# A state-space scan and a low-rank mixer on one core: Up of batches 2 and 3 in blocks of 512 tokens, and a new order of the work

## The chip, the cores and the metric

The kernel runs on one core of a Trainium2 chip. The metric is the device time of one execution in microseconds, the median of several executions. Before the change it is 219.8 us (three runs, 219.1 to 220.63).

## What is computed

The reference has two parts, one fed by the other. There are 4 batches, 8 heads, 768 tokens, head width 32 and state width 16; the mixer's model width is 256, its rank 32 and its hidden width 1024.

```python
# scan, in chunks of 32 tokens
cum = np.cumsum(log_a[:, :, sl], axis=-1)
L = np.exp(cum[:, :, :, None] - cum[:, :, None, :]) * causal
y_intra = (einsum('bhin,bhjn->bhij', C, B) * L) @ x
y_inter = einsum('bhin,bhnd->bhid', C, state) * np.exp(cum)[..., None]
state = exp(sum(log_a)) * state + sum_j(B_j x_j * exp(cum[-1] - cum_j))
y = y_intra + y_inter
# mixer, on y as (batch, token, 256)
h = y^T @ U @ V                      # over tokens, rank 32
u = y + h^T
out = u + max(u @ w_ch1, 0) @ w_ch2  # 256 -> 1024 -> 256: "Up" and "Down"
```

## The kernel before

All engines follow one list, PLAN (line 41). Each word of it is a step, and every step issues its instructions on the engines that it uses, so each engine's queue holds its own share of the steps in the order of the list. A step that waits holds up what lies behind it on its own engine only. `follow` (line 937) reads the list.

The scan works on 12 pieces of 256 tokens, three to a batch, numbered 0 to 11. The words of piece k are: `Bk`, `Xk` loads (with a leading Y where nothing holds them back), `Pk` or `Qk.c` the scaling of B and C by decays on the vector engine (DVE), `Tk` or `Vk...` the transposes on the tensor engine (PE) with their copies on the scalar engine (ACT), `gk` the products C times B (line 544), `mk` and `Mk` the causal mask on DVE (a tile M), `sk` the products for the state (line 578), `uk` the state's update on DVE and its masked copy on GpSimd (POOL), `ik` the part that comes in from earlier pieces (line 658), `nk` and `jk` the part inside the piece (line 694), `yk` the copy out, `tk` or `Ok` the transposes back into token order (line 721).

The mixer's words carry the batch b: `pb`, `qb`, `ab.j` make the low-rank part and add it. The channel mixer then works in blocks of tokens. Before the change every block has 384 tokens, two to a batch. `Sb.j` splits the block's u into three parts (one ACT and two DVE instructions); `fb.j.m` is Up: for one of 8 groups of 128 hidden channels it makes 6 products (3 parts by 2 halves of the width) of 384 columns in a bank of PSUM, which ACT reads once with a relu; `hb.j.m` reads the same bank once on DVE and, at every odd m, joins two results with a DVE instruction of 768 columns; `db.j.k.n` is Down: 4 products of 256 columns, six such words for each 128 tokens of the block, the last with one product more and the sum and the store of the output. The products of Up and Down are issued at line 809. Block 0 of batch 0 is done in plain fp32 (`U`, and four `d` words to 128 tokens).

Weights come in with `w`, `YU`, `YV`, are converted by `c` and `C`, and split by `R`. `v0` (`spread`, line 893) lays V out over the partitions with 16 small products.

`E` words issue fill products (line 140), which compute nothing that is used: `En` is n times a product of a 128-wide identity with itself in fp32, in a bank of its own that it takes in its turn. One instruction covers up to four such units. I call one n a unit below.

PSUM has eight banks; the string BANKS names the bank for each use in turn. SLOTS does the same for 15 scratch tiles in SBUF of 1024 words a partition (`words`), in which loads, conversions, and the results of Up live. A bank or a slot is taken again only when its last reader is done. The loads are issued from SyncE's queue (SP).

Of the kernel before, what the change touches and what calls it, by code (L numbers as in the profile page):

```python
# [15 lines left out]
PLAIN = 1  # L16
BANKS = (
    '01720345670012367400561273334612337423057406175233406175234061752304237562137054713054762167'
    '2305417351473512603512476305143051247626241762405761357204615304712530471240653206127346126731'
    '26705706254317062705647031520312304504153761021072016325040375403')  # L20
SLOTS = (
    'abcdefghijklmnocaefbdgihmecjbldkagofhimncjekandeblmneogmfcmhjiakdbnolefhmgcadjnbeilofkhjcmdeal'
    'gibfonmkjeclhbagfidnkomlej')
# [55 lines left out]
def kernel(  # L79
# [113 lines left out]
    a_sb = const.tile([NB * NH * NC // 2, 2, P], FP32)  # L193
# [46 lines left out]
    Vn = const.tile([P, NC * RK], FP32R)  # L240
    Vs = const.tile([P, S], FP32R)
# [67 lines left out]
    ones = const.tile([P, P], FP32)  # L309
# [18 lines left out]
    upto = triangle("upto", const.tile([P, P], FP32, name="upto"), [[1, P]], 0, -1)  # L328

    low = [triangle("low", const.tile([P, P], FP32, name=f"low{v}"), [[0, P]], 31 + 64 * v, -1)  # L330
# [3 lines left out]
    ref = const.tile([P, P], FP32)  # L334
# [10 lines left out]
    nc.gpsimd.tensor_copy(out=spot, in_=same[:, None, :].to_broadcast([P, 4, Q]))  # L345
    mine = const.tile([P, NH], FP32)
# [19 lines left out]
    middle = const.tile([P, P], FP32)  # L366
    vector.tensor_tensor(out=middle, in0=low[1], in1=low[0], op=ALU.subtract)
    high = const.tile([P, P], FP32)
# [4 lines left out]

    F = const.tile([P, NB, NPR, NH, 2, 2], FP32)
# [28 lines left out]
    def keep(bs, tag="w"):  # L403
# [9 lines left out]
        own = att.tile([P, NB, J, NH], FP32, tag="own", name="own", bufs=1)[:, :n]  # L413
# [322 lines left out]

    def mixer(b):
        uT = yT[b]
        ps = mix.tile([P, DM], FP32R, tag="ps", name="ps")
        hold = {}  # L740
# [38 lines left out]

        def block(n, k):  # L780
            return uT[:, n, ts(k, HS)]
# [17 lines left out]
        def split(j):  # L799

            u = uT[:, :, ts(j, HS)]
            t = mix.tile([P, 3, NCB, HS], FP32R, tag="u", name="u", bufs=1)
            us[j] = [t[:, i] for i in range(3)]
            nc.scalar.activation(us[j][0], u, AF.Copy, scale=NEAR)
            halves(*us[j], u)
# [7 lines left out]
        def pair(dtype):  # L813
            t = words()
            return t.bitcast(dtype)[:, :2 * HS].rearrange("p (m t) -> p m t", m=2)

        def plain(j, m):

            if (j, m // 2) not in gT:
                gT[j, m // 2] = pair(FP32)  # L820
            t = bank("xz"[m % 2], HS)
            products(t, [(w1f[m // 2][:, n, ts(m % 2, P)], block(n, j)) for n in range(NCB)], True)
            nc.scalar.activation(gT[j, m // 2][:, m % 2], t, AF.Relu, scale=1.0 / MORE)

        def up(j, m):

            if (j, m // 2) not in gs:
                gs[j, m // 2] = [pair(FP32R)]
            gs["t", j, m] = t = bank("xz"[m % 2], HS)
            products(t, [(w1[v][:, n, ts(m, P)], us[j][v][:, n])  # L830
                         for v in range(3) for n in range(NCB)], True)
            gs["of", j, m] = behind["turn"]
            nc.scalar.activation(gs[j, m // 2][0][:, m % 2], t, AF.Relu, scale=NEAR)  # L833

        def third(j, m):

            g = gs[j, m // 2]
            if len(g) == 1:
                g.append(pair(FP32R))
# [5 lines left out]
            if m % 2:  # L845
                g.append(pair(FP32R))
                joined(*g)

        def down(j, k, n):

            parts = b or j >= PLAIN
            pieces = 6 if parts else 4
# [4 lines left out]
            if n == 0:  # L857
                gs["o", j, k] = bank("xzx"[k], DM)
            t = gs["o", j, k]
            c = HS // P * j + k  # L860
            if parts:
# [3 lines left out]
            else:  # L865
                products(t, [(gT[j, n][:, m, ts(k, P)], w2f[n][:, m]) for m in range(2)], n == 0)
            if n == pieces - 1:
                products(t, [(Vs[:, ts(c, P)], ps)], False)
                o = ytok[b][:, c]
                stored.append(c)  # L870
                if b < NB - 1 or len(stored) < NC:
                    behind.setdefault("part", summed(o, t, o))
                    nc.sync.dma_start(out=out[b, ts(c, P)], in_=o)
                else:
                    for queue, cols in ((nc.sync, ts(0, P)), (nc.scalar, ts(1, P))):
                        summed(o[:, cols], t[:, cols], o[:, cols])
                        queue.dma_start(out=out[b, ts(c, P), cols], in_=o[:, cols])

        us, gs, gT, stored = {}, {}, {}, []
# [6 lines left out]

    def convert(c, scalar=False):

        if c not in steps:
            steps[c] = to_fp32(*weights[c], c - 2 - NQ, scalar)  # L890
        next(steps[c])

    def spread():

        nc.scalar.copy(out=Vn, in_=Vq)
        vector.tensor_tensor(out=Vq, in0=Vq, in1=Vn.bitcast(FP32), op=ALU.subtract)
        v = [bank(tag, NC * RK) for tag in "yyxz"]
        for q in range(4):
            for i in range(4):
                rows = ts(i, Q)  # L900
                nc.tensor.matmul(out=v[i][ts(q, Q)], lhsT=ident[rows, rows],
                                 rhs=Vq[rows] if q % 2 else Vn[rows].bitcast(FP32),
                                 start=True, stop=True, skip_group_check=True)
# [88 lines left out]
```

## Time and profile before

| | |
|---|---|
| median of three runs | 219.8 us |
| profiled execution, its own time | 221.66 us |
| span of the profiled execution | 219.9 us |
| mean granted clock of the tensor engine | 0.977 |
| PE busy | 211.3 us (96%) |
| DVE busy | 150.1 us (68%) |
| ACT busy | 87.6 us (40%) |
| POOL busy | 35.4 us (16%) |
| read from and written to memory | 10.98 MB, 3.15 MB |

The span runs from the first to the last instruction. A busy share on PE counts an instruction from its start to a modelled end, so many small products that overlap can fill a stretch without the array being full; how densely PE works is seen better in the steps from the start of one product to the start of the next. The granted clock is the share of full speed at which the array ran.

### The profile page before, as it was taken

The numbers are of one execution on the slowest core, as the hardware profiler recorded it, in microseconds if no ns is written. First come the engines' busy times: TensorE is split into PE (matmuls) and PEld (weight loads), VectorE is DVE, ScalarE is ACT, GpSimd is POOL, SyncE is SP. The second block draws the span as 40 slices with busy tenths as digits, with TensorE's granted clock in tenths as the row PEclk, the third lists the DMA queues.
The fourth block names the chain that finished last, engine by engine and source line by source line (L and its number), as shares of the span: only waits on it lengthen the run. The fifth ranks groups of instructions, "written<-read, shape, count | busy, mean of one in ns | idle before, by whom it ended". The sixth has DMA issues, their size and how long they took to land.

```text
span 219.9 us, 7021 instructions
## 1 busy us (share of the span) xinstructions
PE 211.3 (96%) x3058; PEld 186.8 (85%) x3058; DVE 150.1 (68%) x314; ACT 87.6 (40%) x196; POOL 35.4 (16%) x52
## 2 busy tenths in 40 slices
PE   7879989998999999999999999999999999999994
PEld 3646756666778989999999988999999999999993
DVE  4737796787768899789653779746518776647532
ACT  2342736567574555443053531236342222323000
POOL 3011023368570740001000101200000000000000
PEclk9965999999999999999999999999999999999999
DMA  5989584678686850203210301000000000100012
GB/s 94 107 121 133 121 139 110 143 217 216 135 117 118 132 62 3 48 16 82 29 51 3 72 3 48 30 3 1 3 0 24 30 23 0 48 16 11 0 53 93
DMA packets 69663, 14.58 MB, mean 66 GB/s; under 512 B 63808, under 2 KB 67840, under 8 KB 69632
## 3 DMA queue, kind: packets, MB, share of 16 engines
q1 hardware_dynamic: 69488, 14.06, 32.6%
q8 instruction: 24, 0.39, 0.8%
q10 hardware_dynamic: 144, 0.07, 0.1%
q14 instruction: 7, 0.06, 0.1%
HBM read 10.98 MB, written 3.15 MB: 64 GB/s over the span
## 4 chain that ended last, share of the span: by engine, by line
PE 86%; DVE 6%; SPq 3%; DMA 1%; issue 1%; POOL 1%; DVEq 0%; POOLq 0%
PE x L809 38%; PE z L809 27%; PE y L694 4%; SPq L210 3%; PE y L658 3%; PE x L544 2%; PE w L504 2%; DVE words L182 2%; PE w L721 2%; PE w L140 2%; DMA bc<-in_C_dram 1%; PE w L578 1%; DVE M L182 1%; DVE S L182 1%; PE w L747 1%
## 5 line engine op out<-in xcount | busy, mean ns | idle before, releaser
L182 DVE SCALAR_TENSOR_TENSOR words<-words 128x768 fp32r<-128x768 f32 (+3 forms) x39 | 35.9, 919 | 5.1 <-PE z L809 3.4
L809 PE MATMUL x<-w,words 128*128 128x256 f32 x224 | 34.4, 284 | 0.0
L809 PE MATMUL x<-u,w 128*128 128x384 f32 x168 | 33.9, 340 | 0.0
L809 PE MATMUL z<-u,w 128*128 128x384 f32 x168 | 33.0, 340 | 0.0
L833 ACT ACTIVATE words<-x 128x384 fp32r<-128x384 f32 x28 | 13.8, 492 | 44.0 <-PE x L809 43.9
L809 PEld LDWEIGHTS x<-w,words 128*128 128x128 f32 x224 | 30.5, 190 | 0.2 <-issue 0.2
L809 PEld LDWEIGHTS z<-u,w 128*128 128x128 f32 x168 | 29.1, 188 | 0.3
L809 PEld LDWEIGHTS x<-u,w 128*128 128x128 f32 x168 | 28.8, 188 | 0.4 <-issue 0.2
L809 PE MATMUL x<-w2c,words 128*128 128x256 f32 x144 | 25.2, 305 | 0.0
L833 ACT ACTIVATE words<-z 128x384 fp32r<-128x384 f32 x28 | 13.7, 491 | 25.3 <-PE z L809 25.3
L809 PEld LDWEIGHTS x<-w2c,words 128*128 128x128 f32 x144 | 21.1, 189 | 1.1 <-issue 0.4
L182 DVE SCALAR_TENSOR_TENSOR words<-z,words 128x384 fp32r<-128x384 f32 x28 | 15.4, 551 | 9.0 <-ACT words L833 8.9
L809 PE MATMUL z<-w,words 128*128 128x256 f32 x112 | 18.4, 287 | 0.0
L182 DVE SCALAR_TENSOR_TENSOR words<-x,words 128x384 fp32r<-128x384 f32 x28 | 14.9, 551 | 4.0 <-ACT words L833 3.8
L605 POOL TENSOR_TENSOR Sm<-S,own 128x256 f32<-128x256 f32 (+1 forms) x12 | 7.2, 602 | 61.6 <-DVE S L182 61.6
L809 PEld LDWEIGHTS z<-w,words 128*128 128x128 f32 x112 | 15.7, 190 | 0.2
L694 PEld LDWEIGHTS y<-M,x 64*32 64x32 f32 x768 | 8.7, 113 | 5.9 <-POOL settled L617 2.8
L694 PE MATMUL y<-M,x 64*32 64x64 f32 x768 | 12.0, 237 | 1.5 <-POOL settled L617 1.3
L809 PE MATMUL z<-w2c,words 128*128 128x256 f32 x72 | 13.2, 307 | 0.0
L182 DVE SCALAR_TENSOR_TENSOR S<-S,kept,w 128x64 f32<-128x64 f32 x40 | 11.2, 280 | 2.6 <-PE w L504 0.5
L182 DVE TENSOR_TENSOR M<-x,causal 128x256 int32<-128x256 int32 x24 | 9.0, 416 | 5.7 <-PE z L544 4.3
L182 DVE SCALAR_TENSOR_TENSOR ytok<-x,ytok 128x256 f32<-128x256 f32 (+1 forms) x17 | 6.8, 407 | 7.3 <-PE x L809 7.3
(137 smaller groups left out, 337.3 us busy)
## 6 DMA issues: line engine op xcount, KB each, us to landing
words<-in_moe_w_ch_dram SPq DMA_DIRECT2D x7, 512.0 KB, 5.3
x<-in_x_dram SPq DMA_DIRECT2D x24, 128.0 KB, 3.2
out_dram<-ytok SPq DMA_DIRECT2D x23, 128.0 KB, 1.7
bc<-in_B_dram SPq DMA_DIRECT2D x24, 64.0 KB, 3.2
bc<-in_C_dram SPq DMA_DIRECT2D x12, 128.0 KB, 3.3
words<-in_moe_w_ch_dram SPq DMA_DIRECT2D x2, 256.0 KB, 3.0
words<-in_moe_U_dram SPq DMA_DIRECT2D x1, 192.0 KB, 3.5
words<-in_moe_V_dram SPq DMA_DIRECT2D x4, 48.0 KB, 2.5
```

The source lines that it names most:

```text
L140: nc.tensor.matmul(out=t[:, :m * P].rearrange("p (m i) -> p m i", i=P), lhsT=ident, rhs=ident[:, None, :].to_broadcast([P, m, P]), start=T ...
L182: self.last = call(*args, **kwargs)
L210: op = issuer[0].dma_start(**kwargs)
L504: nc.tensor.transpose(out=tp[:, i, v], in_=s["BC"][:, i, c + v].rearrange("p h n -> p (h n)"), identity=ident)
L544: nc.tensor.matmul(out=s["g"][r][cols, c], lhsT=s["T"][rows, 0, c, cols], rhs=s["Cm"][rows, :, :, ts(2 * c + p, Q)].rearrange("r v t i -> ...
L578: nc.tensor.matmul(out=s["A"][p][ts(r, Q), v], lhsT=s["BC"][half, 0, v, 2 * r:2 * r + 2].rearrange("p h n -> p (h n)"), rhs=x_sb[k][half, ...
L605: nc.gpsimd.tensor_tensor(out=s["Sm"][:, sl], in0=s["S"][:, sl].rearrange("p i (s d) -> p i s d", s=2), in1=own2[:, b, 4 * q + sl.start:4 ...
L658: nc.tensor.matmul(out=channels(k)[r // 2][ts(r % 2, H), c, p], lhsT=own[ts(r, Q)], rhs=st[k]["T"][ts(r, Q), 1, :, ts(2 * c + p, Q)].rearr ...
L694: product = nc.tensor.matmul(out=y[n][ts(i, Q), c, p], lhsT=x_sb[k][half, c, h], rhs=s["M"][half, h // 2, c, h % 2], start=fresh(k, n, [i] ...
L721: nc.tensor.transpose(out=t[:, c, g], in_=yT[b][:, g, ts(2 * q + c, P)], identity=ident)
L809: nc.tensor.matmul(out=t, lhsT=lhsT, rhs=rhs, start=start, stop=True, skip_group_check=True)
L833: nc.scalar.activation(gs[j, m // 2][0][:, m % 2], t, AF.Relu, scale=NEAR)
```

## The change

The list and the strings of banks and slots are new as a whole. Both openings, up to the first word of Up:

```python
# before
    'YX0 A0 YB0 Q0.0 YB1 A1 Q0.2 Q0.1 K0 s0 YB2 YB3 Q1.0 V0.0.0 V0.1.1 Q1.2 YU0 YX1 Q1.1 u0 '
    'Q2.0 E1 Q2.2 g0 m0 V1.0.2 B5 M0 V1.1.2 w0 V2.0.2 E2 n0 j0 g1 YX2 YV0 m1 i0 E1 P3 E1 M1 Q2.1 c0 '
    's1 n1 u1 c0 T3 T3 E2 V2.1.3 c1 P5 j1 y0 i1 g2 m2 w1 O0.0 s2 c1 B4 y1 T5 u2 M2 T5 g3 C0 m3 i2 '
    'n2 E1 X3 c0 j2 M3 y2 C0 c2 t1 C0 w3 c2 O2.1 v0 p0 s3 P4 T4 u3 X4 q0 c2 w2 T4 g5 a0.0 M5 X5 c4 '
    'w5 m5 n3 c1 U0.0.1 U0.0.0 ...'
# after
    'YX0 YB0 A1 A0 E1 Q0.0 YB1 E2 Q0.2 Q0.1 V0.0.0 V0.1.1 YX1 Q1.0 K0 YB2 s0 Q1.2 g0 E1 V1.0.2 Q1.1 '
    'm0 YX2 V1.1.2 s1 u0 E3 M0 B5 g1 E1 m1 n0 E2 M1 i0 Q2.0 Q2.1 j0 s2 y0 w0 YB3 u1 w1 Q2.2 n1 '
    'V2.0.2 P5 E4 YU0 V2.1.3 u2 YV0 T5 j1 w5 T5 c1 X3 B4 O0.0 g2 m2 i1 M2 i2 y1 P3 t1 c2 T3 c0 E1 '
    'c2 w2 T3 c0 n2 c1 E3 X4 w3 C0 X5 C0 E1 j2 c2 c1 w6 g3 m3 y2 R0 O2.1 E1 C0 E2 v0 c6 M3 c0 p0 g5 '
    'E1 M5 s3 w4 u3 q0 P4 n3 a0.0 i3 T4 m5 c6 R0 T4 U0.0.1 ...'
```

All fill words lie in these stretches: 6 words with 8 units before, 13 words with 23 units after. The words of Up for batches 2 and 3 go from 32 `f` words to 24, and their splits from four to three. The other words are the same ones in a new order, apart from the numbering of `d` words, of which there are 138 in both. The rest of the diff:

```diff
+BLOCKS = {(2, 0): [(2, 0, 512)], (2, 1): [(2, 512, 256), (3, 0, 256)], (3, 0): [(3, 256, 512)]}
...
-    a_sb = const.tile([NB * NH * NC // 2, 2, P], FP32)
+    early_on = [words().bitcast(FP32) for n in range(2)]
+    squares = iter([early_on[0][:, ts(n, P)] for n in range(8)])
+    a_sb = early_on[1][:NB * NH * NC // 2, :2 * P].rearrange("r (g s) -> r g s", g=2)
...
+    Vf = const.tile([P, NC * RK], FP32R)
...
-    ones = const.tile([P, P], FP32)
+    ones = next(squares)
...      (upto, low, ref, middle, high in the same way; own goes into early_on[1])
+    spread_to = const.tile([P, 2, 4, Q], FP32R)
...
+        def parts(j):
+            return BLOCKS.get((b, j), [(b, j * HS, HS)])
+
+        def wide(j):
+            return sum(n for own, first, n in parts(j))
...
         def split(j):
-            u = uT[:, :, ts(j, HS)]
-            t = mix.tile([P, 3, NCB, HS], FP32R, tag="u", name="u", bufs=1)
+            t = mix.tile([P, 3, NCB, 4 * P], FP32R, tag="u", name="u", bufs=1)[:, :, :, :wide(j)]
             us[j] = [t[:, i] for i in range(3)]
-            nc.scalar.activation(us[j][0], u, AF.Copy, scale=NEAR)
-            halves(*us[j], u)
+            at = 0
+            for own, first, n in parts(j):
+                u = yT[own][:, :, first:first + n]
+                to = [v[:, :, at:at + n] for v in us[j]]
+                nc.scalar.activation(to[0], u, AF.Copy, scale=NEAR)
+                halves(*to, u)
+                at += n
...
-                gs[j, m // 2] = [pair(FP32R)]
-            gs["t", j, m] = t = bank("xz"[m % 2], HS)
+                gs[j, m // 2] = [pair(FP32R, wide(j))]
+            gs["t", j, m] = t = bank("xz"[m % 2], wide(j))
...
-                gs["o", j, k] = bank("xzx"[k], DM)
+                gs["o", j, k] = bank("xzxz"[k], DM)
...
+    def apart_of():
+        nc.gpsimd.tensor_copy(out=spread_to.rearrange("p n q r -> p (n q) r"),
+                              in_=none[:, None, :].to_broadcast([P, 8, Q]))
+        for n in range(2):
+            nc.gpsimd.tensor_copy(out=spread_to[:, n].rearrange("p (q two) r -> p two q r", two=2)[:, n],
+                                  in_=same[:, None, :].to_broadcast([P, 2, Q]))
...
     def spread():
         nc.scalar.copy(out=Vn, in_=Vq)
-        vector.tensor_tensor(out=Vq, in0=Vq, in1=Vn.bitcast(FP32), op=ALU.subtract)
+        vector.tensor_tensor(out=Vf, in0=Vq, in1=Vn.bitcast(FP32), op=ALU.subtract)
         v = [bank(tag, NC * RK) for tag in "yyxz"]
-        for q in range(4):
+        for n, part in enumerate((Vn, Vf)):
             for i in range(4):
                 rows = ts(i, Q)
-                nc.tensor.matmul(out=v[i][ts(q, Q)], lhsT=ident[rows, rows],
-                                 rhs=Vq[rows] if q % 2 else Vn[rows].bitcast(FP32),
-                                 start=True, stop=True, skip_group_check=True)
+                nc.tensor.matmul(out=v[i], lhsT=spread_to[rows, n].rearrange("p q r -> p (q r)"),
+                                 rhs=part[rows], start=n == 0, stop=True, skip_group_check=True)
```

The middle block of the three, (2, 1), takes the last 256 tokens of batch 2 and the first 256 of batch 3, so its split reads two tiles, and its words wait for both batches. The constants that only the opening needs no longer have tiles of their own: they lie in the first two scratch slots. The outputs and the other steps of the mixer (in `down`, whose token counting now goes by `tokens` and `stored`) are as before.

More of the change, by code (lines that the diff above doesn't have):

```diff
@@ L17 @@
 BANKS = (
-    '01720345670012367400561273334612337423057406175233406175234061752304237562137054713054762167'
-    '2305417351473512603512476305143051247626241762405761357204615304712530471240653206127346126731'
-    '26705706254317062705647031520312304504153761021072016325040375403')
+    '0120200034567120334713356422033564722107253172066665342666017526304417350417042610742354261507'
+    '2670661570615703547235610562310476547106523123061307230527436105271437132174321043705342175621'
+    '75621324573204573206173456120457321475143514714305747627647506')
 SLOTS = (
-    'abcdefghijklmnocaefbdgihmecjbldkagofhimncjekandeblmneogmfcmhjiakdbnolefhmgcadjnbeilofkhjcmdeal'
-    'gibfonmkjeclhbagfidnkomlej')
+    'abcdefghijklmnobagcfkdhoemgijkbodlenamfcgjkhicjkhlboeklendkmajgfhocbiedlnamkhjgodfcilebanmkjhd'
+    'giobakgfclemnjoi')
+BLOCKS = {(2, 0): [(2, 0, 512)], (2, 1): [(2, 512, 256), (3, 0, 256)], (3, 0): [(3, 256, 512)]}
 NEAR = 1.0 - 2.0 ** -13
@@ L326, in triangle @@
         return out
-    upto = triangle("upto", const.tile([P, P], FP32, name="upto"), [[1, P]], 0, -1)
-    low = [triangle("low", const.tile([P, P], FP32, name=f"low{v}"), [[0, P]], 31 + 64 * v, -1)
+    upto = triangle("upto", next(squares), [[1, P]], 0, -1)
+    low = [triangle("low", next(squares), [[0, P]], 31 + 64 * v, -1)
            for v in range(2)]
-    ref = const.tile([P, P], FP32)
+    ref = next(squares)
     vector.memset(ref, 0.0)
@@ L364 @@
     nc.scalar.activation(la, la, AF.Ln)
-    middle = const.tile([P, P], FP32)
+    middle = next(squares)
     vector.tensor_tensor(out=middle, in0=low[1], in1=low[0], op=ALU.subtract)
-    high = const.tile([P, P], FP32)
+    high = next(squares)
     vector.tensor_tensor(out=high, in0=ones, in1=low[1], op=ALU.subtract)
@@ L372 @@
                             axis=mybir.AxisListType.X, op=ALU.add)
+    none = const.tile([P, Q], FP32)
+    nc.gpsimd.memset(none, 0.0)
     F = const.tile([P, NB, NPR, NH, 2, 2], FP32)
@@ L412, in keep @@
         J = 2 * NC - 1
-        own = att.tile([P, NB, J, NH], FP32, tag="own", name="own", bufs=1)[:, :n]
+        own = early_on[1][:, 2 * P:2 * P + n * J * NH].rearrange(
+            "p (b j h) -> p b j h", b=n, h=NH)
         vector.tensor_tensor(
@@ L734, in ytokens @@
             pass
+    shares, stored = {}, {}
     def mixer(b):
@@ L739, in mixer @@
         ps = mix.tile([P, DM], FP32R, tag="ps", name="ps")
+        shares[b] = ps
         hold = {}
@@ L778, in added, with tokens @@
                 behind.setdefault("part", summed(u, t, u))
+        def parts(j):
+            return BLOCKS.get((b, j), [(b, j * HS, HS)])
+        def wide(j):
+            return sum(n for own, first, n in parts(j))
+        def tokens(j, k):
+            at = k * P
+            for own, first, n in parts(j):
+                if at < n:
+                    return own, (first + at) // P
+                at -= n
         def block(n, k):
@@ L799, in split @@
         def split(j):
-            u = uT[:, :, ts(j, HS)]
-            t = mix.tile([P, 3, NCB, HS], FP32R, tag="u", name="u", bufs=1)
+            t = mix.tile([P, 3, NCB, 4 * P], FP32R, tag="u", name="u", bufs=1)[:, :, :, :wide(j)]
             us[j] = [t[:, i] for i in range(3)]
-            nc.scalar.activation(us[j][0], u, AF.Copy, scale=NEAR)
-            halves(*us[j], u)
+            at = 0
+            for own, first, n in parts(j):
+                u = yT[own][:, :, first:first + n]
[3 more added lines that the diff above has]
+                at += n
         def products(t, pairs, start):
@@ L811, in products, with pair @@
                 start = False
-        def pair(dtype):
+        def pair(dtype, n):
             t = words()
-            return t.bitcast(dtype)[:, :2 * HS].rearrange("p (m t) -> p m t", m=2)
+            return t.bitcast(dtype)[:, :2 * n].rearrange("p (m t) -> p m t", m=2)
         def plain(j, m):
             if (j, m // 2) not in gT:
-                gT[j, m // 2] = pair(FP32)
+                gT[j, m // 2] = pair(FP32, HS)
             t = bank("xz"[m % 2], HS)
@@ L838, in third @@
             if len(g) == 1:
-                g.append(pair(FP32R))
+                g.append(pair(FP32R, wide(j)))
             near, far = g[:2]
@@ L845, in third @@
             if m % 2:
-                g.append(pair(FP32R))
+                g.append(pair(FP32R, wide(j)))
                 joined(*g)
         def down(j, k, n):
-            parts = b or j >= PLAIN
-            pieces = 6 if parts else 4
+            whole = not b and j < PLAIN
+            pieces = 4 if whole else 6
             def weight(v, m):
@@ L857, in down @@
             if n == 0:
-                gs["o", j, k] = bank("xzx"[k], DM)
+                gs["o", j, k] = bank("xzxz"[k], DM)
             t = gs["o", j, k]
-            c = HS // P * j + k
-            if parts:
+            if whole:
+                products(t, [(gT[j, n][:, m, ts(k, P)], w2f[n][:, m]) for m in range(2)], n == 0)
+            else:
                 v, half = divmod(n, 2)
@@ L864, in down @@
                              for m in range(NQ * half, NQ * half + NQ)], n == 0)
-            else:
-                products(t, [(gT[j, n][:, m, ts(k, P)], w2f[n][:, m]) for m in range(2)], n == 0)
             if n == pieces - 1:
[L868 to L871, printed above, removed]
+                own, c = tokens(j, k)
+                products(t, [(Vs[:, ts(c, P)], shares[own])], False)
+                o = ytok[own][:, c]
+                stored[own] = stored.get(own, 0) + 1
+                if own < NB - 1 or stored[own] < NC:
                     behind.setdefault("part", summed(o, t, o))
-                    nc.sync.dma_start(out=out[b, ts(c, P)], in_=o)
+                    nc.sync.dma_start(out=out[own, ts(c, P)], in_=o)
                 else:
@@ L876, in down @@
                         summed(o[:, cols], t[:, cols], o[:, cols])
-                        queue.dma_start(out=out[b, ts(c, P), cols], in_=o[:, cols])
-        us, gs, gT, stored = {}, {}, {}, []
+                        queue.dma_start(out=out[own, ts(c, P), cols], in_=o[:, cols])
+        us, gs, gT = {}, {}, {}
         return SimpleNamespace(p=project, q=parted, a=added, S=split, f=up, h=third, d=down,
@@ L885 @@
     steps = {}
+    def apart_of():
[4 more added lines that the diff above has]
+                                  in_=same[:, None, :].to_broadcast([P, 2, Q]))
     def convert(c, scalar=False):
         if c not in steps:
+            if c < 0:
+                apart_of()
             steps[c] = to_fp32(*weights[c], c - 2 - NQ, scalar)
```

63 rows, old and new, of the table PLAN are left out of this document.

## The prediction

> **What bounds the kernel now.** I read the page's busy shares and clock first, then a table of stages cut where the clock and the kind of work change, then the chain of work that ended last inside the weak stage.
>
> ```profile
> PE 211.3 (96%) x3058; PEld 186.8 (85%) x3058; DVE 150.1 (68%) x314; ACT 87.6 (40%) x196; POOL 35.4 (16%) x52
> PEclk9965999999999999999999999999999999999999
> PE 86%; DVE 6%; SPq 3%; DMA 1%; issue 1%; POOL 1%; DVEq 0%; POOLq 0%
> ```
>
> PE is busy 96% of the span and makes 86% of the chain. The clock row has a dip near the start and nowhere else. The stages:
>
> ```profile
> core 0: us, PE busy (x) PEld busy (x) DVE busy (x) ACT busy (x) POOL busy (x), PEclk, DMA share, GB/s
> 0.00:7.20 7.20, 6.08 (x25) 3.23 (x26) 3.06 (x13) 2.33 (x4) 2.06 (x12) 1.00 0.67 94
> 7.20:12.70 5.50, 3.72 (x78) 2.41 (x78) 4.90 (x16) 3.13 (x12) 0.95 (x2) 1.00 0.91 111
> 12.70:22.90 10.20, 9.60 (x230) 6.54 (x229) 4.96 (x17) 2.44 (x7) 0.97 (x3) 0.50 0.90 138
> 22.90:37.20 14.30, 13.43 (x407) 8.88 (x391) 11.17 (x34) 9.09 (x26) 3.63 (x7) 1.00 0.56 115
> 37.20:50.00 12.80, 12.80 (x270) 8.20 (x270) 10.69 (x29) 6.30 (x13) 6.34 (x7) 1.00 0.73 177
> 50.00:80.00 30.00, 29.45 (x413) 24.86 (x413) 24.26 (x42) 19.51 (x41) 16.89 (x16) 1.00 0.76 139
> 80.00:216.70 136.70, 136.22 (x1694) 132.64 (x1670) 90.54 (x167) 44.78 (x94) 4.51 (x8) 1.00 0.10 26
> 216.70:219.90 3.20, 0.00 (x0) 0.00 (x0) 0.49 (x2) 0.00 (x0) 0.00 (x0) 1.00 0.27 85
> ```
>
> From 37.2, where the first word of Up starts, PE is idle 0.55 us up to 80 and 0.48 us in the 136.7 us behind it. A new order can gain almost nothing there; only less PE work can. The last 3.2 us are the last sum and store, the same words in both lists. What is loose is the opening: between 12.7 and 22.9 PE ran at half clock, and no other engine was busy more than 4.96 of the 10.2 us. (The Trainium skill, "TensorE: Matmul & The Clock Gate", Part 1, says that the array's clock has two states, full and half, that it falls to half after a window of some 3.4 us without enough work and rises after a busy one; 0.50 over 10.2 us, three such windows, agrees.) The chain through this stage:
>
> ```profile
> 8.35 3.26 DMA bc<-in_C_dram
> 11.63 0.50 DVE BC L182
> ...
> 12.51 1.09 PE w L140 x2
> 13.64 0.76 PE y L694 x32
> ...
> 14.70 0.68 PE y L694 x32
> ...
> 17.11 0.74 PE w L140 x2
> 17.89 0.81 PE w L140 x2
> 18.74 0.68 PE w L578 x32
> ...
> 19.95 1.04 PE w L504 x4
> 21.00 0.87 PE w L140 x2
> ...
> 36.61 0.48 PE y L694 x32
> ...
> 37.18 0.88 PE z L809 x2
> ```
>
> It comes in by a load of C (for piece 2), and then stays on PE. The fills (line 140) take 1.09 + 0.74 + 0.81 + 0.87 = 3.5 us of it, the rest 6.7. The same 32 products of line 694 take 0.68 to 0.76 here and 0.48 at full clock. The 6.7 us are so some 3.35 us at full clock.
>
> **The change part by part, Up in 512.** The step from one product to the next is read from starts, not durations:
>
> ```profile
> 179.83 1.22 PE L809 MATMUL x<-u,w 128*128 128x384 f32 x6
> 180.89 0.64 PE L809 MATMUL x<-w,words 128*128 128x256 f32 x4
> 181.37 2.27 PE L809 MATMUL z<-u,w 128*128 128x384 f32 x12
> 183.48 0.64 PE L809 MATMUL x<-w,words 128*128 128x256 f32 x4
> 183.95 0.64 PE L809 MATMUL z<-w,words 128*128 128x256 f32 x4
> ```
>
> Twelve products of 384 take 183.48 - 181.37 = 2.11 us, 0.176 each; four of 256 take 0.47 to 0.48, 0.119 each. A third 128 columns therefore cost 0.057, and no fixed part to speak of is left (0.119 - 2 x 0.057 = 0.005). 512 columns, which this trace does not show, come to 0.176 + 0.057 = 0.233 on that line; the other end is the proportional 0.176 x 4/3 = 0.235. Removed: 4 blocks x 48 = 192 products, 33.8 us. Added: 3 x 48 = 144, 33.6 us (33.8 at the other end). Gain 0 to 0.2; I take **-0.2**, the straight line through both rows. The products of Down stay 24 and one more to 128 tokens.
>
> Beside that stands a rule. The Trainium skill, "TensorE: Matmul & The Clock Gate", Part 1, has a warm product cost N / 2.4 GHz plus 2.5 ns whatever its width; that is 0.216 for 512 columns, and by it the sum would lose 33.8 - 144 x 0.216 = 2.7 us instead of 0.2. It would put 384 columns at 0.1625, and the trace has 0.176, so I do not build on it.
>
> **The engines behind Up.**
>
> ```profile
> L833 ACT ACTIVATE words<-z 128x384 fp32r<-128x384 f32 x28 | 13.7, 491 | 25.3 <-PE z L809 25.3
> L729 ACT COPY ytok<-w 128x512 f32<-128x512 f32 x10 | 5.8, 593 | 3.1 <-PE w L721 2.9
> L182 DVE SCALAR_TENSOR_TENSOR words<-z,words 128x384 fp32r<-128x384 f32 x28 | 15.4, 551 | 9.0 <-ACT words L833 8.9
> L182 DVE SCALAR_TENSOR_TENSOR words<-words 128x768 fp32r<-128x768 f32 x28 | 28.0, 1001 | 4.9 <-PE z L809 3.4
> ```
>
> ACT reads 24 banks of 512 at about 0.59 in place of 32 of 384 at 0.49 (14.2 against 15.7 us). DVE's reads cost at most 0.551 x 4/3 = 0.73 each and the joins 1.33, so 24 x 0.73 + 12 x 1.33 = 33.5 against 32 x 0.551 + 16 x 1.0 = 33.6 us, a gain of 0 there and some more if each has a fixed part. Both lie beside PE, which after 80 leaves DVE 46 of 136.7 us free. Cost on the path: 0. Without that cover a bank would come back to PE 0.1 to 0.2 us later. The middle block needs batch 3's `a3.0` before `S2.1`. Between `S2.1` and its first Up lie six words of Down, 6 x 4 x 0.119 = 2.9 us; ACT's and DVE's share of a part of 256 tokens is two thirds of a 384 one, and DVE's sums for `a3.0` (2 x 0.55) come first in its queue, so a wait of 0 to 0.5 us is possible at this one place. The new list also takes some banks right behind the word that frees them (`g6`, `f0.1.3`, `d0.1.2.0`, `s11`). I take **+0.4** for both, ends 0 and 1.5.
>
> **The opening.** The list has 23 fill units where it had 8, all ahead of the first Up. Two units at half clock took 0.87 us (21.00), so one costs 0.43 there and 0.215 at full clock; the 15 more cost 3.2 us of PE at full clock if nothing hides them. The loads are re-ordered in SP's queue:
>
> ```profile
> 8.35 0.66 SPq L210 DMA_DIRECT2D bc<-in_C_dram  x1
> ...
> 13.29 0.58 SPq L210 DMA_DIRECT2D words<-in_moe_U_dram  x1
> 13.92 1.17 SPq L210 DMA_DIRECT2D x<-in_x_dram  x2
> ```
> ```profile
> x<-in_x_dram SPq DMA_DIRECT2D x24, 128.0 KB, 3.2
> ```
>
> X for piece 1 is issued at 13.92 now and lands 3.2 us after its issue, near 18; its products (line 578) start at 18.74, with two fills ahead of them. In the new list it goes out ahead of piece 2's B and C, of which the load at 8.35 is one, so by about 8.5, and is there by about 12. Piece 2's B and C go out two DMAs later, but their scaling (`Q2`) now stands behind piece 0's masks and first products, in DVE's queue too, so the landing at 11.6 no longer holds up the masks of piece 0. U, V and the later loads go out behind. That is 0.5 us of PE idle removed of 5.50 - 3.72 = 1.78 before 12.7 (**-0.5**, ends 0 and 1.5).
>
> Does the clock hold? If it does, the stage of 10.2 us has 3.35 us of PE work without fills and 4.96 us of DVE work. It cannot go under 5.0; the DVE share that the neighbours reach (4.90 of 5.50, 11.17 of 14.30) puts it at 5.5 to 6.4. I take 6.0, so **-4.2**; ends -5.2 and 0. The fills need room: 23 x 0.215 = 4.95 us at full clock, against idle PE of 1.78 before, 6.0 - 3.35 = 2.65 in, and 14.30 - 13.43 = 0.87 after the stage, 5.3 together. They fit by 0.35 us; in a slot where PE would wait they cost nothing, elsewhere 0.215 each.
>
> The rest: `spread` issues 8 products in place of 16. Their number of array passes at 192 columns is not shown here; I bound the step by gaining or losing 0.5 us and take 0. It needs three POOL copies more; `spot`, of the same kind, is
>
> ```profile
> 2.86 0.29 POOL L345 COPY spot<-same 128x128 f32<-128x128 f32 x1 [0.75 <-DVE same L182]
> ```
>
> so about 1 us at twice the width, beside a POOL that is busy 3.63 of 14.3 us; if `v0` had to wait for it, up to 1 us. The constants in scratch slots and the one split less cost nothing on the path: their slots come again as the 16th and 17th of the scratch tiles (`U0.0.1` and the load `w7`), long after the last decay has read them.
>
> **Sum**, against the profiled span of 219.9 (its execution ran 221.66 by its own clock; the median of three runs, 219.8, stands at the span, so I take the span's sum as the median): 219.9 - 0.2 + 0.4 - 0.5 - 4.2 = **215.4**.
>
> **Rivals.**
>
> *The clock falls all the same* (218 to 221, taken 220.2). If PE's share in the window before 12.7 is again too small, the stage stays at 10.2, and the list's ten units from `E3` to `E4` take 4.3 us in it where 3.5 stood: 219.9 + 0.8 - 0.5 - 0.2 + 0.2. For it: 8 units did not hold it. Against it: X is there six us earlier, and 8 of the units, not 3, lie ahead of piece 0's first product of line 694.
>
> *Fills stand ahead of ready work* (slower, 223.5). PE's queue is in order, and a fill also waits for a bank. If the opening is bound by DVE and loads less than I think, the 15 more units are work on the path: at half clock 15 x 0.43 = 6.5, less the 1.78 + 0.87 idle outside the stage that they fill, 3.8; 219.9 + 3.8 - 0.2. It decides as soon as PE's idle time ahead of Up is under the fills' own time. For it: the fit is 0.35 us, and in this profile fills already hold 3.5 us of the chain.
>
> *512 columns cost clearly less than the line* (213.2). For it: weight loads are busy 132.64 of the 136.7 us behind 80, so a part of each step may be a load that does not hide, and 48 loads go. Against it: the rows of 256 and 384 leave a fixed part of 0.005. Between that and a whole step of 0.119 I price it at 0.05: 48 x 0.05 = 2.4 in place of 0.2. The rule of the Trainium skill quoted above ("TensorE: Matmul & The Clock Gate", Part 1) would make it 2.7.
>
> **How the numbers follow.** My forecast, the clock holds and fills fit, has 0.55 (own range 213.5 to 217.4, from a stage of 5.0 to 7.5 us with the other ends); the wide products 0.10; the clock falls 0.18; fills in the way 0.17. A difference of about 1%, 2.2 us, is what these runs can tell from none. Faster 0.55 + 0.10 = 0.65, same 0.18, slower 0.17. The range 212.5 to 221 takes in all but the last rival.
>
> **What would show it.** In the profile after: granted clock 1.00 between 12.7 and 22.9, or at half for one window at most; the first Up at 32 to 34 in place of 37.2; from it to PE's end 179 us as now (216.7 - 37.2 = 179.5); products of 384 at 0.176 and of 512 near 0.233 from start to start; fills of 0.2 us that no one in the chain waits for; 3.2 us behind PE's end. It is wrong if Up starts at 36 or later, if chain rows of line 140 exceed 3.5 us, or if the stretch from Up to the end grows by more than a microsecond.

## The result, and the profile after

The change made the kernel slower: 228.32 us (226.81 to 228.5) against 220.22 us for the kernel before, ratio 1.035 (95% interval 1.029 to 1.041). The profiled execution has a span of 226.5 us, 6.6 more than the one before; the times differ by more, 8.1 us, because the profile of before is of one of its longer executions (221.66 us, granted clock 0.977). The page's lines that answer to those shown of before, and the stages with the same first cuts (columns: window, its length, busy time of PE, weight loads, DVE, ACT and POOL with their counts, granted clock, DMA share, GB/s):

```profile
PE 214.4 (95%) x3000; PEld 181.2 (80%) x3000; DVE 151.4 (67%) x302; ACT 86.1 (38%) x188; POOL 37.5 (17%) x55
PEclk9998599999799999999999999999999999999999
PE 84%; DVE 6%; issue 3%; DMA 2%; SPq 2%; POOL 1%; ACT 0%; DVEq 0%; POOLq 0%
```
```profile
7.20:12.70 5.50, 5.13 (x114) 3.37 (x112) 4.68 (x16) 3.20 (x11) 0.59 (x2) 1.00 0.94 128
12.70:22.90 10.20, 7.29 (x223) 4.67 (x223) 6.18 (x20) 1.92 (x6) 2.75 (x8) 0.93 0.87 146
22.90:37.20 14.30, 13.97 (x308) 10.01 (x306) 8.51 (x28) 8.68 (x24) 2.86 (x5) 0.81 0.88 185
37.20:50.00 12.80, 12.00 (x229) 8.09 (x232) 11.09 (x27) 6.75 (x15) 6.30 (x6) 1.00 0.66 196
50.00:80.00 30.00, 27.29 (x363) 21.03 (x355) 21.32 (x34) 15.75 (x33) 12.88 (x12) 0.94 0.47 74
```

The clock did hold between 12.7 and 21, as forecast, and the time did not come. In 12.7 to 22.9 PE is busy 7.29 us instead of 9.60: it waits. The clock then falls twice, from 21.4 for 6.8 us and near 59 for 3.4 us, 10.2 us in all, as much as before, but later. The stage 50 to 80, which PE had filled to 0.55 us, has 2.7 us of idle PE. Where the two waits are, `j1` and `j4`, by the timeline (start, length, engine, line, what, and in brackets the idle time before it and what ended it; line numbers are those of each kernel's own file: 701 here was 694, 836 was 809, 624 was 617, 454 was 447):

```profile
19.02 0.69 DVE L182 TENSOR_TENSOR BC<-bc,F 128x512 f32<-128x512 f32 x1 [1.96 <-DMA bc<-in_B_dram]
...
19.77 0.44 PE L511 MATMUL w<-ident,BC 128*128 128x128 f32 x2 [0.96 <-DVE BC L182]
...
20.15 0.91 DVE L182 SCALAR_TENSOR_TENSOR S<-S,kept,w 128x64 f32<-128x64 f32 x3
...
21.14 0.51 POOL L612 TENSOR_TENSOR Sm<-S,own 128x192 f32<-128x192 f32 x1 [3.60 <-DVE S L182]
...
21.59 0.25 POOL L624 COPY settled<-slot 128x1 f32<-128x1 f32 x1
...
21.89 0.68 PE L701 MATMUL y<-M,x 64*32 64x64 f32 x32 [1.68 <-POOL settled L624]
```
```profile
57.25 1.35 POOL L454 TENSOR_TENSOR w1f<-words 128x512 int32<-128x512 int32 x1 [1.48 <-ACT yT L719]
58.55 0.38 POOL L624 COPY settled<-slot 128x1 f32<-128x1 f32 x1
...
58.98 0.68 PE L701 MATMUL y<-M,x 64*32 64x64 f32 x32 [2.71 <-POOL settled L624]
```

A word `jk` has to stand apart from its `nk`: PE may begin it only when another engine has done an instruction that waited for PE's work of `nk` or behind it. If no DVE instruction of that kind has come between them, `intra` puts a copy of one column, `settled`, on POOL and lets PE wait for it. The copy needs only `nk`, but POOL's queue is in order. At `j1` (21.89) it lay behind the masked copy of `u2`, that behind DVE's update, that behind a transpose's copies, and DVE had stood still 1.96 us for the load of piece 5's B, which the new list asks for here. At `j4` (58.98) the list has the end of conversion `c5` between `n4` and `j4`, so the copy lay behind c5's addition, and PE stood 2.71 us. The kernel before had the same shape at its `j4`, where conversion `c6` stood ahead; its copy came out in time for all but 0.55 us:

```profile
48.55 1.61 POOL L447 TENSOR_TENSOR w2c<-words 128x512 int32<-128x512 int32 x1 [1.89 <-PE w L578]
50.11 0.38 POOL L617 COPY settled<-slot 128x1 f32<-128x1 f32 x1
...
50.55 0.86 PE L694 MATMUL y<-M,x 64*32 64x64 f32 x64 [0.55 <-POOL settled L617]
```

The clock of the changed kernel right behind its wait, by windows:

```profile
55.00:59.00 4.00, 1.29 (x8) 0.41 (x7) 3.93 (x6) 1.80 (x5) 2.44 (x3) 0.99 0.73 114
59.00:62.40 3.40, 3.40 (x39) 2.69 (x40) 3.37 (x5) 1.22 (x3) 1.51 (x2) 0.51 0.57 77
```

So this wait is paid twice: PE's idle time, and then 3.4 us of a busy PE at half clock. (The Trainium skill, "TensorE: Matmul & The Clock Gate", Part 1, has the clock fall after an idle window of about 3.4 us; the stretch of 3.4 us at half clock behind the wait agrees with that length, but 2.7 us of idle were enough here.)

The first Up:

```profile
40.12 1.46 PE L836 MATMUL z<-yT,w1f 128*128 128x384 f32 x4
```

In sums: the first Up starts at 40.12 (37.18 before), 2.9 us later. From there to the end of PE's last product it is 183.1 us (179.5 before), 3.6 more. Behind it are 3.3 us (3.2 before).

### The profile page after: what moved, and what is told of

Read it like the earlier page. It is cut to its first block, busy times and chain, and to the rows that moved or that the text cites. A ratio compares the mean times of both kernels' runs of the same rounds, so it can differ in the third digit from the quotient of the medians.

```text
span 226.5 us, 6884 instructions
## 1 busy us (share of the span) xinstructions
PE 214.4 (95%) x3000; PEld 181.2 (80%) x3000; DVE 151.4 (67%) x302; ACT 86.1 (38%) x188; POOL 37.5 (17%) x55
## 4 chain that ended last, share of the span: by engine, by line
PE 84%; DVE 6%; issue 3%; DMA 2%; SPq 2%; POOL 1%; ACT 0%; DVEq 0%; POOLq 0%
PE x L836 34%; PE z L836 28%; PE x L551 3%; PE y L701 3%; PE y L665 2%; PE w L728 2%; PE w L511 2%; PE w L140 2%; DVE words L182 2%; PE w L585 1%; SPq L212 1%; DVE u L182 1%; DMA bc<-in_B_dram 1%; DVE S L182 1%; DVE M L182 1%
## 5 line engine op out<-in xcount | busy, mean ns | idle before, releaser
L182 DVE SCALAR_TENSOR_TENSOR words<-words 128x768 fp32r<-128x768 f32 (+4 forms) x35 | 33.8, 971 | 1.6
L836 PE MATMUL x<-u,w 128*128 128x384 f32 (+1 forms) x144 | 33.3, 371 | 0.4 <-DVE M L182 0.3
L836 PE MATMUL z<-u,w 128*128 128x384 f32 (+1 forms) x144 | 33.2, 368 | 0.0
L836 PE MATMUL x<-w,words 128*128 128x256 f32 x192 | 28.3, 285 | 0.0
L860 ACT ACTIVATE words<-x 128x384 fp32r<-128x384 f32 (+1 forms) x24 | 13.0, 545 | 34.5 <-PE x L836 26.8
L836 PEld LDWEIGHTS x<-w,words 128*128 128x128 f32 x192 | 25.1, 188 | 0.4
L182 DVE SCALAR_TENSOR_TENSOR words<-x,words 128x384 fp32r<-128x384 f32 (+1 forms) x24 | 14.5, 620 | 16.5 <-ACT words L860 16.4
L860 ACT ACTIVATE words<-z 128x384 fp32r<-128x384 f32 (+1 forms) x24 | 13.1, 547 | 26.9 <-PE z L836 26.9
L182 DVE SCALAR_TENSOR_TENSOR words<-z,words 128x384 fp32r<-128x384 f32 (+1 forms) x24 | 14.8, 617 | 5.2 <-ACT words L860 5.0
L836 PEld LDWEIGHTS z<-w2c,words 128*128 128x128 f32 x88 | 13.5, 195 | 1.0
```

The lines of the kernel that those rows point to most:

```text
L182: self.last = call(*args, **kwargs)
L836: nc.tensor.matmul(out=t, lhsT=lhsT, rhs=rhs, start=start, stop=True, skip_group_check=True)
```

## The experiments

All are the changed kernel with words of its list moved or left out, unless said otherwise; where fill words went, the banks that they took went too, and in e13 and e14 one bank is dealt out anew. Ratios are to the kernel before, timed beside each run, with their 95% intervals. Three readings of the loss are set against each other: the queue theory (PE waits for the POOL copy, and the clock falls behind the wait), the fill theory (the 15 more fill units lie on PE's path) and the width theory (blocks of 512 are slower).

**The two waits: e1, e2, e3.** e1 moves one word:

```diff
-n4 c7 c5 U0.0.5 y5 X7 c5 c5 j4
+n4 c7 c5 U0.0.5 y5 X7 j4 c5 c5
```

> The changed kernel with one word moved: j4, which waits for a small POOL copy, stands ahead of the last two words of conversion c5 and not behind them, so that the copy stands ahead of c5's 1.35 us POOL addition. Queue theory (the loss is PE waiting for that copy behind POOL work, and the half clock that follows each such wait): the 2.7 us idle at 55.8 us goes to under 0.6, the half-clock window at 48 to 63 us goes too, and the time falls by 2.2 to 4 us from 228.3 to 224.3 to 226.1 (ratio to the kernel before 1.018 to 1.027). Fill theory (the loss is the 15 more fill units on PE's path): no change, 227.5 to 228.5. Width theory (blocks of 512 are slower): no change.

Measured 223.21 us, 1.012 (1.008 to 1.016): 5.1 us less. In its timeline the copy now stands ahead of c5's addition (`w1f`), and PE's products of `j4` follow without idle time:

```profile
52.55 1.62 POOL L453 TENSOR_TENSOR w2c<-words 128x512 int32<-128x512 int32 x1 [0.68 <-issue]
54.12 0.39 POOL L623 COPY settled<-slot 128x1 f32<-128x1 f32 x1
54.61 0.29 PEld L700 LDWEIGHTS y<-M,x 64*32 64x32 f32 x32 [0.55 <-POOL settled L623]
54.61 0.46 PE L700 MATMUL y<-M,x 64*32 64x64 f32 x32
...
55.66 1.35 POOL L453 TENSOR_TENSOR w1f<-words 128x512 int32<-128x512 int32 x1 [1.15 <-DVE words L181]
```

From the first Up to PE's end it takes 178.8 us instead of 183.1. In this profile the clock is full throughout (mean 1.000), in the opening too, which the moved word cannot touch; there it starts Up at 38.53 and not at 40.12. Whether the wait at `j1` pulls the clock down thus differs between executions, and a part of the 5.1 us can be that. The granted clocks of the timed executions allow a closer comparison. The changed kernel's shortest, 226.81 us, had 0.992, which is one stretch of 3.4 us; if that is the one behind `j4`, its opening had none, as in e1's two executions at 1.000, which took 222.34 and 222.38. Its other three had 0.976 to 0.977, two stretches more, and took 228.19 to 228.5; e1's two with 0.985, two stretches, took 224.13 and 224.28. So the moved word alone is worth some 4.2 to 4.5 us, an estimate from these few executions. Only the queue theory allowed for a gain; it had said 2.2 to 4 us, and too little.

e2 moves piece 5's step out of the way of `u2` and `j1`, and e3 does both:

```diff
-V2.0.2 P5 E4 YU0 V2.1.3 u2 YV0 T5 j1 w5 T5
+V2.0.2 E4 YU0 V2.1.3 u2 YV0 j1 P5 T5 w5 T5
```

> The changed kernel with P5 and the first T5 moved behind u2 and j1, so that DVE's u2, and with it the POOL copy that j1 waits for, no longer stand behind the late load of B for piece 5. Queue theory: the idle of 0.96 and 1.68 us of PE between 18.6 and 21.9 us shrinks to under 1 us in all, the clock does not fall at 21.4 us (or falls for one window instead of two), the first Up starts 2 to 4 us earlier than 40.1, and the time falls by 2 to 4 us, to 224.3 to 226.3. Fill theory: at most the idle itself comes back, 1.6 us, to 226.7 or more. Width theory: no change.

> Both moves at once. Queue theory: the two gains add, 4 to 8 us, to 220.3 to 224.3, which is the kernel before or up to 2% over it; what is left over it are the fills. Fill theory: 226 to 228. Width theory: 226 to 228.

Measured 226.79 us, 1.027 (1.018 to 1.035), and 222.65 us, 1.009 (1.006 to 1.013). e2's step is a miss: `j1` starts at 21.82, with 2.68 us of idle PE ahead of it. With the load gone from DVE's queue the next in line held the copy up: fill `E4` (1.02 us of PE), behind it `V2.1.3`, behind that DVE's update and POOL's masked copy. What lay behind what was right, what came last was not. Its time is not clear of the changed kernel's, whose interval it overlaps. Its profiled opening ran at full clock and has Up at 38.41, as e1's has it at 38.53 with `P5` in the old place, so the move itself gave 0.1 us. e3 lies in its forecast of 220.3 to 224.3, but by e1's word: the intervals of the two overlap.

**The copy ahead of u2, and the fills: e7, e8, e9, e4.** e7 is e1 with `j1` itself ahead of `u2`; e8 is e7 without the six fill words behind `E4` (9 of 23 units), e9 is e7 without any; e4 takes the same 9 units out of the changed kernel as it is.

```diff
-V2.0.2 P5 E4 YU0 V2.1.3 u2 YV0 T5 j1 w5 T5
+V2.0.2 E4 YU0 V2.1.3 j1 u2 YV0 P5 T5 w5 T5
```

> The changed kernel with j4 ahead of the end of c5 as in e1_j4, and j1 moved ahead of u2 (with P5 and its transposes behind), so that the POOL copy that j1 waits for no longer stands behind u2's masked copy. Queue theory: j1 starts at 19 to 19.5 us and not at 22, the idle of 1.7 to 2.7 us ahead of it is gone, the first Up starts 2 to 2.7 us earlier than in e1_j4 (38.5), and the time is 220.3 to 221.5 (e1_j4 223.2). Fill theory: the idle moves to another place and the time stays at 222.5 to 223.5.

> As e7_j1_ahead, without the six fill words behind E4 (9 units; 14 are left). Fill theory: each unit is 0.215 us of PE's path, so 1.9 us less than e7_j1_ahead. Cover theory of the prediction: they lie in waits, no change (under 0.5 us). Clock theory: without them the clock falls for one or two windows of 3.4 us, up to 1.7 us slower for each.

> As e7_j1_ahead, without any fill word. Fill theory: 23 units, up to 4.9 us less than e7_j1_ahead where all of them lie on the path. Clock theory: the clock is at half for 10 us or more between 9 and 25 us, and the time is that of e8_14units or up to 3 us more. Cover theory: as e8_14units within 0.5 us if the clock costs nothing in this stage.

> The changed kernel as it is, without the six fill words behind E4 (9 units, 1.9 us of PE at full clock). Fill theory: 1.5 to 2 us less than 228.3. Cover theory (the opening is bound elsewhere): under 0.6 us less, and the waits at j1 and j4 are as in the changed kernel.

| | time | ratio | first Up | Up to PE's end |
|---|---|---|---|---|
| after | 228.32 | 1.035 (1.029 to 1.041) | 40.12 | 183.1 |
| e7 | 221.52 | 1.003 (0.999 to 1.007) | 37.49 | 178.8 |
| e8, 14 units | 220.68 | 0.999 (0.995 to 1.003) | 37.07 | 178.8 |
| e9, none | 221.17 | 1.001 (0.997 to 1.005) | 37.78 | 178.8 |
| e4 | 227.33 | 1.029 (1.023 to 1.034) | 39.66 | 183.3 |

`j1` starts at 19.09 in e7, as the queue theory said, but only 1.0 of the 2 to 2.7 us that it forecast reaches the first Up (38.53 to 37.49); 1.7 us come back as a wait for piece 5 at `T5`:

```profile
19.09 0.45 PE L700 MATMUL y<-M,x 64*32 64x64 f32 x32
...
21.28 0.66 PE L510 MATMUL w<-ident,BC 128*128 128x128 f32 x4 [1.74 <-DVE BC L181]
```

With both waits mended the time shows no difference to the kernel before. That does not make the two lists equal: e7's five executions with a granted clock of 0.997 or more took 221.0 to 223.1 us, where the kernel before, in its 39 executions at such a clock, took 219.0 to 221.0.

Now the fills. 9 units are 1.9 us of PE; without them Up starts 0.4 us earlier (e8, whose opening has one stretch of 3.4 us at half clock where e7's has none) or 0.5 (e4). The times fall by 0.8 (e8 against e7) and 1.0 us (e4 against after), and in both pairs the intervals overlap; e4 lies between the forecast of the fill theory, 1.5 to 2 us, and that of the cover theory, under 0.6. Without any fill PE has 4.9 us less to do and starts Up no earlier: it waits instead, and two stretches of 3.4 us at half clock appear ahead of the first Up. The fills do not make the loss, and they buy nothing that can be measured.

**The code and the width: e5, e6.** e5 has the changed code with the list, banks and 384-blocks of before, and its slots behind two new ones for the constants; e6 has the list of before up to the first split of batch 2 and then the words of the new list with three blocks of 512.

```diff
-BLOCKS = {(2, 0): [(2, 0, 512)], (2, 1): [(2, 512, 256), (3, 0, 256)], (3, 0): [(3, 256, 512)]}
+BLOCKS = {}
...      (and PLAN, BANKS of the kernel before, SLOTS with two letters ahead: e5)
```

> The code of the changed kernel (constants in scratch slots, the new spread, the new helpers) with the list, the banks and the slots of the kernel before and all blocks of 384 tokens. If the loss is in the order of the list, as all three theories have it in different ways, this runs as the kernel before, 219 to 221 us (ratio 0.995 to 1.005), less up to 0.5 us where spread costs less. If the moved constants or the new spread cost something, it is slower by that, up to 1 us.

> The order of the kernel before up to its first split of batch 2, and from there the rest of the words in the order of the changed kernel, with three blocks of 512; banks and slots behind the cut are dealt out least recently released first. This is the width alone, in the changed code. Width theory (512 is slower): over the kernel before by some us. Line reading of the prediction: 0.2 to 0.4 us less PE work, so 219.5 to 221.5 with the kernel before at 221.3, ratio 0.99 to 1.00; the last product at 0 to 1 us earlier than 216.7.

Measured 221.42 us, 1.001 (0.997 to 1.005), and 221.55 us, 1.001 (0.997 to 1.005). Neither the moved constants, nor the new `spread`, nor the blocks of 512 cost or gain what can be measured. In e6 the last two of the six products in the first bank of Up of batch 2 came about 1 us late, for the split on DVE (starts at 141.94 and 143.86, with four products, 0.92 us, between them), and that stood against the blocks' small gain. The step of a 512 product, in the timeline of the changed kernel:

```profile
204.19 1.56 PE L836 MATMUL x<-u,w 128*128 128x512 f32 x6
205.58 1.54 PE L836 MATMUL z<-u,w 128*128 128x512 f32 x6
206.96 0.64 PE L836 MATMUL z<-w2c,words 128*128 128x256 f32 x4
```

Six take 1.38 to 1.39 us, 0.231 each, where the line through 256 and 384 gave 0.233. (The 0.216 of the Trainium skill, "TensorE: Matmul & The Clock Gate", Part 1, is under it by 0.015.)

**What bounds the opening: e10, e11, e13, e14.** In e9's chain of work that ended last, a load comes in late:

```profile
17.68 2.19 SPq L211
...
20.55 4.91 DMA words<-in_moe_U_dram
25.48 0.57 DVE words L181 x3
```

So e10 (from e8) and e11 (from e9) load U, V and the first weights ahead of piece 5; e13 (from e8) and e14 (from e10) move `P5` and `T5` behind pieces 0 and 1.

```diff
-M0 B5 g1 ... y0 w0 YB3 ... YU0 V2.1.3 j1 u2 YV0 P5 T5 w5 T5 c1 X3
+M0 YU0 YV0 w0 g1 ... y0 B5 YB3 ... V2.1.3 j1 u2 w5 c1 P5 T5 T5 X3
```

> As e8_14units, with the loads of U and V and the first w_ch1 load moved ahead of the loads of piece 5, and P5 with its transposes behind c1. Load theory (the opening is bound by when U and V land: they are issued at 20.5 us and converted on DVE, which PE's clock and fills do not change): U lands before 18 us, c0 and spread run 1 to 3 us earlier, the first Up starts at 34.5 to 36.2 (37.1 in e8_14units) and the time is 218.0 to 219.8. Clock and fill theory: the first Up stays at 37 and the time at 220.2 to 221.2. DVE theory (the opening is DVE's work in a row): no change either, since that work is the same.

> As e9_no_fills, with the same loads moved. Load theory: the first Up starts at 34.5 to 36.5 (37.8 in e9_no_fills), the time is 218.5 to 220. Clock theory: half-clock windows stay and now cost, 220.5 to 221.5. Against e10_uv_14units it shows what 14 fill units are worth in an opening that no longer waits for loads.

> As e8_14units, with P5 (which waits for a load of B) and its transposes T5 moved from behind j1 to behind piece 0's and 1's y copies, and one bank re-dealt. Place theory (DVE and PE wait at P5 and T5 for that load, with everything else behind them in their queues): the 1.8 us idle ahead of T5 at 21 us goes and the first Up starts 0.8 to 1.8 us earlier than 37.1; 219 to 220.2 us. Load theory (U and V set the opening): the idle goes to the conversions, the first Up stays at 36.8 to 37.3, 220.3 to 221.3.

> As e10_uv_14units (U, V and w loads ahead of piece 5's), with P5 and T5 moved the same way. Place theory: the wait of 4.7 us at T5 that made e10 slow goes whole, first Up at 35 to 37 (41.0 in e10), 218.5 to 220.5 us. If the first Up comes at 35 to 36, loads and place together were the bound of the opening; if it stays over 38, the loads of piece 5 are needed as early as the changed list has them, wherever P5 stands.

Measured: e10 224.37 us, 1.020 (1.016 to 1.024); e11 223.33 us, 1.016 (1.011 to 1.020); e14 224.22 us, 1.016 (1.011 to 1.021). All three are slower than every time forecast for them. U was issued earlier, at 13.77 in e10 and 20.61 in e8, but PE stood for piece 5, as e10's waits have it (total, times, longest):

```profile
PE w L510 <- DVE BC L181: 4.7, 1, 4.7
```

Up starts at 41.0, 40.3 and 40.5. e14, where that wait was moved out of the way, has waits of 0.7 to 2.1 us in five places of its opening. By its own forecast, Up behind 38 means that piece 5's loads are needed as early as the changed list has them. e13 (222.13 us, 1.002, 0.995 to 1.009) spreads from 219.91 to 224.43 and says nothing either way. The openings of e10, e11 and e14 also ran 6.8, 10.2 and 10.2 us at half clock, where e8's ran 3.4, so a part of their loss may be the clock. What bounds the opening is not shown; that several chains are late by about the same is my reading of it.

**A split moved ahead: e12.** From e10, against 0.9 us that PE loses at `f1.0.2` in all kernels with the new list:

```diff
-h0.1.3 n6 g7 i6 j6 m7 S1.0 y6
+h0.1.3 S1.0 n6 g7 i6 j6 m7 y6
```

> As e10_uv_14units, with the split S1.0 ahead of the masks and copies of piece 6 and 7 and not behind them, so that its two DVE instructions do not end after PE reaches f1.0.2. In all kernels with the new list PE lost 0.9 us there. Queue theory: that 0.9 us goes, the time is 0.5 to 1 us under e10_uv_14units. Rival (the wait is for the bank or DVE's work as a whole, and moves to the mask of piece 7): no change.

Measured 228.1 us, 1.037 (1.033 to 1.042), 3.7 us slower than e10. The rival had the mechanism, the wait moved to the masks of piece 7, but it had said no change. The split's DVE work now stands ahead of piece 7's masks, and PE waits for those in a place where Down needs their banks:

```profile
PE x L835 <- DVE M L181: 3.4, 1, 3.4
```

A stretch of 3.4 us at half clock follows that wait too, from 86.8 to 90.2.

**The list before with both: e15.** The order of before, with its own small wait at `j4` taken out in the same way and the first split of batch 2 in its old place, then the three blocks of 512:

```diff
-n4 w7 c6 s5 U0.0.2 j4
+n4 w7 s5 U0.0.2 j4 c6
```

> The order of the kernel before up to and with its first split of batch 2, with j4 ahead of the end of c6 (its POOL copy then stands ahead of c6's POOL addition), then the changed kernel's order with three blocks of 512. Width and queue theory: e6's wait of 1.1 us at f2.0.1 and the 0.8 us at j4 go, the blocks give 0.2 to 0.4 us; PE ends at 214.5 to 215.5, the time is 1 to 2 us under the kernel before, ratio 0.991 to 0.996. If the waits move elsewhere: ratio 0.997 to 1.003.

Measured 219.72 us, 0.999 (0.996 to 1.003): no difference that shows, and the gain of 1 to 2 us that I expected is a miss. Its profiled execution ran at full clock all through, with a span of 217.4 us; the timed ones lie between 218.6 and 222.3. Its first Up, and below it that of e1, also at full clock:

```profile
35.16 1.53 PE L835 MATMUL z<-yT,w1f 128*128 128x384 f32 x4
```
```profile
38.53 1.46 PE L835 MATMUL z<-yT,w1f 128*128 128x384 f32 x4
```

It is the version to keep if one is kept, for its shorter list, not for its time.

## Why the prediction was wrong, step by step

**The stage at half clock (-4.2) failed, and with it the sum.** I took the work on PE's chain between 12.7 and 22.9 as bound by the clock, because the chain stays on PE. In the changed kernel the clock held to 21.4, and PE waited instead: it is busy 7.29 of the 10.2 us. The same opening, from before's list, starts Up at 37.18 with 10.2 us at half clock, at 36.81 with 3.4 us (e5) and at 35.16 with none (e15). The whole clock is worth 2.0 us there, half of what I gave it. The times say the same. Of 82 executions of the kernel before, timed beside the experiments, 39 had a granted clock of 0.997 or more and took 219.9 us on average; 13 had 0.977, as in the profile, and took 221.5. So I priced a dip that many executions do not have. I also set the profiled span, 219.9, equal to the median time, 219.8, but that execution's own time was 221.66: what I took 4.2 us off was already near the time without the dip. And the two openings compare at equal clock as 35.16 (e15) and 38.53 (e1): the new order is 3.4 us longer by itself. Of that the copy at `j1` is 1.0 (e7) and the late fills about 0.4 (e8); the rest, 2 us, has not been pinned to one cause. In sum, Up starts 7.6 us behind the 32.5 of the forecast (37.2 - 0.5 - 4.2), the stretch behind it is 3.4 us over its 179.7 (179.5 - 0.2 + 0.4), and time over span is 1.8 (228.32 - 226.5), together the 12.9 us between 215.4 and 228.32 but for 0.1.

**The loads (-0.5) came as described and did not pay.** The state products of piece 1 start at 11.02 instead of 18.74, and PE's idle time from 7.2 to 12.7 falls from 1.78 to 0.37 us; the first Up is later all the same. I did not price the lateness of piece 5's B, though `P5` stands ahead of `u2` on DVE in the list as printed; by e2 it was not what came last at `j1`, and in e7 it is a wait of 1.7 us behind it.

**The waits in the dense part (+0.4) were the wrong waits.** I went through banks, splits and DVE, and stopped at engines that work on data. The 2.7 us at `j4` come from a POOL copy that exists only to hold PE back. Before's trace had shown it: PE's wait for `settled` was 1.3 us in three places there, and the list shows `c5 c5` ahead of `j4`. The half clock behind the wait belongs to this term too: from Up to PE's end the changed kernel takes 4.3 us more than e1 (183.1 and 178.8), 1.6 more than the wait.

**Fills in the way**, the rival that came out nearest in its time, had the wrong mechanism: 9 of the 23 units cost 0.4 to 1 us of the 8, if that is not noise, and leaving out all 23 gained nothing that can be measured (e9 against e7), where 3.8 was forecast. **The clock falls all the same** was half right: 10.2 us at half in both, but in other places. **The width (-0.2)** was right in its size, 0.231 against 0.233, DVE's reads at 0.685 and joins at 1.225 were under the bounds of 0.73 and 1.33, and the wider reading cost PE nothing. **The rest** held: 3.3 us behind PE's end, and 178.8 us from Up on once `j4` was mended, where I had said 179.

## What to carry to other kernels

When a list is re-ordered, follow every engine's queue past the words that only hold something back, such as a copy used as a barrier: what is queued ahead of it on its own, mostly idle engine decides when the busy one goes on. Look at several executions, and at what an engine does at half clock, before pricing the clock: if it goes on to wait for a load or another engine, the clock is worth only what is left behind the last of these waits (here 2.0 us for 10.2 at half). And a wait of about 3 us in a dense stretch of PE costs about half as much again: behind those of 2.7 us (the changed kernel) and 3.4 us (e12) the clock went down for 3.4 us.

## What the runs showed of the hardware

The state of the clock in the opening is not a property of the program alone. Up to the first Up, e1 and the changed kernel have the same words; the opening ran at full clock in e1's profiled execution and at half clock for 6.8 us in the changed kernel's, and Up came at 38.53 and 40.12. Up to PE's end, the stretches at half clock were 3.4 us or a multiple of it in every profile: 3.4 in e3, e5 and e8, 6.8 in e10, 10.2 in the kernel before. In the time of one and the same kernel this is worth some 0.8%: 219.9 and 221.5 us for the kernel before at a granted clock of 0.997 or more and of 0.977.
